# Attention followed by a two-layer Mish network: the first layer of the last two token groups as seven products in place of eight

## The chip, the core and the metric

The kernel runs on one core of one Trainium2 chip. TensorE (PE) multiplies matrices and writes its results to PSUM, which has eight banks; VectorE (DVE), ScalarE (ACT) and GpSimd (POOL) work on tiles; SyncE (SP) issues DMA transfers. Every engine runs its own instructions in order and waits on semaphores for the others. The metric is the device time of one execution in microseconds. All times below are microseconds unless another unit stands beside them.

## What is computed

Linear attention with a decay per head, in blocks of 64 positions, on 4 batches, 8 heads, 768 positions and 64 channels; its output, rearranged to 3072 tokens of 512 channels, goes through a network 512 to 2048 to 512 with the Mish function between the layers:

```python
for b in range(nb):                                  # blocks of 64 positions
    intra = np.einsum('bhic,bhjc->bhij', qb, kb) * Dmask[None]
    intra = np.einsum('bhij,bhjd->bhid', intra, vb)
    inter = np.einsum('bhid,bhde->bhie', qb * lam_pow[None], kv_state)
    out[:, :, sl] = intra + inter
    kv_state = lam_block[None, :, None, None] * kv_state + np.einsum('bhsd,bhse->bhde', kb_dec, vb)
...
x = np.ascontiguousarray(attn_out.transpose(0, 2, 1, 3)).reshape(B * S, H * D)
h = x @ w_in                                         # (3072, 512) @ (512, 2048)
sp = np.where(h > 20.0, h, np.log1p(np.exp(np.minimum(h, 20.0))))
g = h * np.tanh(sp)
return (g @ w_out).astype(np.float32)                # (3072, 2048) @ (2048, 512)
```

## The kernel before

The positions are cut into six groups of 128 (n = 0 to 5); a group has 512 tokens, 128 of each batch. Three things are done for a group, each in a later stage than the one before: attention, the first layer with Mish, and the second layer. The order of all instructions is written out by hand, and each engine and each DMA queue takes its own in that order.

**Attention of a group** goes by batch b. `scores` (L246) multiplies the transposed keys and queries kT and qT into the banks be and bo, and DVE multiplies them by the decay mask into two tiles sb (L255). `outputs` (L267) multiplies the queries by the running state and the masked scores by the values into bank bz; DVE scales that into xn (L279), and SP transposes xn by DMA into xt (L282), the input of the first layer, with tokens along its free side. `state` (L294) renews the running state: PE into bank be, DVE adds (raw, L305), POOL multiplies (L307). `turn_dma` (L235) makes kT and qT of two batches by DMA transposes; the tiles rotate over three buffers each. `load_pair` (L84) loads k, q, v, issued by POOL.

**First layer.** A `unit` (L332) makes 128 of the 2048 hidden features of a group: four matmuls over the 512 inputs, weights of win as the stationary side, 512 tokens moving (L324), into one of the banks bA, bB, bC in turn; ACT applies Mish from there into hsg (L330). A group has 16 units. The weights lie in four tiles win[0] to win[3], each with 512 of the features. For group 1, `two_units` (L343) does the same with 256 tokens at a time.

**Second layer.** For groups 1 to 5 it is done with seven products in place of eight: tokens, hidden features and output features are cut in halves, and sums of quarters (`token_sum`, L379, on the activations; `weight_sum`, L366, on the weights wout) are multiplied instead of the quarters. `dense2` (L437) does the products in the order 1, 2, 6, 5, 7, 3, 4, each as two half products of eight matmuls with 256 columns (L431), in the banks bG and bH: the value after product 1 is copied by ACT from bG to bH and grows on in both, and ACT and DVE make the four output quarters from them. `dense2_alone` (L489) does it for the last group, with more banks and nothing beside it.

**The loop** (L715, n = 1 to 4) interleaves, on PE, the attention of group n+2 (`s_` for the scores, `o_` for outputs and state), the 16 units of group n+1 (`u`) and the half products of group n (`h`). In turn n = 3 the last attention, of group 5, is done, without a new state; turn n = 4 has no attention. The last two half products that a turn calls already belong to the group after. The tail after the loop is `dense2_alone` for group 5.

## Time and profile before

| | |
|---|---|
| median of 3 runs | 210.7 us (210.14 to 212.43) |
| profiled execution | 210.12 us, its span 208.4 us |
| instructions in the span | 4263 |
| mean granted TensorE clock | 0.994 |

The span reaches from the first to the last instruction that the profile shows; the rest of the time lies around it. In rows of groups the numbers are the busy time, the mean duration in ns of one instruction, and the idle time of the engine just before them with what ended it. In rows of the timeline they are start, duration, engine, line and operation; the idle time before stands in brackets. In rows of stretches they are the length, then busy time and instruction count of each engine, the granted TensorE clock, the share of the DMA engines, and GB/s. Consecutive matmuls overlap: in the timeline a run of them is shown longer than the distance to the next one's start; the chain of waits shows that distance.

### The profile page before, as it was taken

What the parts mean: (1) busy time and instruction counts of PE and PEld (TensorE: products, weight loads), DVE (VectorE), ACT (ScalarE), POOL (GpSimd) and SP (SyncE); (2) the same over time, 40 slices, a digit from 0 to 9 for tenths busy, and PEclk for the clock granted to TensorE, in tenths of its full rate; (3) what the DMA queues carried; (4) which work ended last, traced back from release to release, by engine and by line L of the source; (5) the groups of instructions that cost most, each with busy time, mean ns of one, the idle gap of its engine ahead of it and who ended that gap; (6) DMA issues with size and microseconds to landing.
All of it is one profiled execution on the core that took longest, in us unless ns stands there. A gap on an engine that the chain in (4) does not pass through costs nothing.

```text
span 208.4 us, 4263 instructions
## 1 busy us (share of the span) xinstructions
PE 196.9 (94%) x1783; PEld 134.1 (64%) x1783; DVE 124.9 (60%) x201; ACT 89.4 (43%) x154; POOL 70.8 (34%) x68
## 2 busy tenths in 40 slices
PE   7568998999999999999999999999999999999991
PEld 3455555788855566667766657766667666666891
DVE  6656758785957957657965657951638340153341
ACT  4674586648421124442254342344352354525300
POOL 7997553531292540763411665400000000000020
PEclk9999999999999999999999999999999999999997
DMA  9999999999989999999991999992022401012033
GB/s 131 136 170 205 162 179 157 182 206 179 160 95 173 203 150 170 140 146 98 194 265 56 73 116 176 159 234 78 3 25 76 129 0 50 0 53 101 0 104 101
DMA packets 109301, 26.23 MB, mean 126 GB/s; under 512 B 99426, under 2 KB 108770, under 8 KB 109282
## 3 DMA queue, kind: packets, MB, share of 16 engines
q0 software_dynamic: 77536, 13.37, 83.3%
q1 hardware_dynamic: 30704, 12.33, 29.7%
q10 hardware_dynamic: 1042, 0.26, 0.6%
q8 instruction: 14, 0.23, 0.4%
q14 instruction: 5, 0.04, 0.1%
HBM read 27.26 MB, written 6.29 MB: 161 GB/s over the span
## 4 chain that ended last, share of the span: by engine, by line
PE 88%; DMA 4%; POOL 2%; ACT 2%; DVE 1%; issue 1%; POOLq 0%; DVEq 0%
PE bG L431 15%; PE bH L431 13%; PE bA L324 11%; PE bB L324 11%; PE bC L324 11%; DMA qn<-in_q_dram 3%; PE be L251 3%; PE bB L350 3%; PE bz L271 2%; PE bz L276 2%; PE bA L350 2%; PE bC L350 2%; PE bA L482 2%; PE bG L482 2%; PE bC L482 2%; PE bB L482 2%
## 5 line engine op out<-in xcount | busy, mean ns | idle before, releaser
L324 PEld LDWEIGHTS <-win 128*128 128x128 f16 x328 | 30.5, 98 | 24.0 <-issue 1.0
L307 POOL TENSOR_TENSOR w<-raw,lbm 128x512 f16<-128x512 f32 x14 | 20.4, 1458 | 53.7 <-DVE raw L305 53.7
L431 PEld LDWEIGHTS <-gsum 128*128 128x128 f16 x336 | 30.9, 98 | 7.3
L431 PEld LDWEIGHTS <-hsg 128*128 128x128 f16 x240 | 23.4, 98 | 7.8
L324 PE MATMUL bA<-xt,win 128*128 128x512 f16 (+2 forms) x112 | 27.9, 371 | 0.6 <-ACT xt L265 0.6
L324 PE MATMUL bC<-xt,win 128*128 128x512 f16 x108 | 27.7, 379 | 0.0
L255 DVE TENSOR_TENSOR sb<-be,dm 128x512 f16<-128x512 f32 x23 | 15.8, 688 | 18.8 <-PE bo L251 18.8
L324 PE MATMUL bB<-xt,win 128*128 128x512 f16 (+2 forms) x108 | 26.9, 371 | 0.0
L330 ACT ACTIVATE hsg<-bA 128x512 f16<-128x512 f32 x27 | 16.1, 597 | 24.4 <-PE bA L324 24.4
L330 ACT ACTIVATE hsg<-bB 128x512 f16<-128x512 f32 x26 | 15.5, 598 | 23.6 <-PE bB L324 23.6
L279 DVE TENSOR_TENSOR xn<-bz,lq 128x512 f16<-128x512 f32 x20 | 13.8, 692 | 18.9 <-PE bz L276 18.9
L330 ACT ACTIVATE hsg<-bC 128x512 f16<-128x512 f32 x27 | 16.2, 598 | 20.3 <-PE bC L324 20.2
L513 POOL TENSOR_TENSOR u<-u,u 128x512 f32<-128x512 f32 x1 | 1.3, 1274 | 64.2 <-DVE u L512 64.2
L431 PE MATMUL bH<-tsum,gsum 128*128 128x256 f16 x160 | 20.4, 273 | 0.0
L431 PE MATMUL bG<-wout,hsg 128*128 128x256 f16 x160 | 20.2, 272 | 0.0
L394 DVE TENSOR_TENSOR gsum<-hsg 128x1024 f16<-128x1024 f16 x20 | 15.1, 753 | 6.4 <-ACT hsg L330 6.4
L255 DVE TENSOR_TENSOR sb<-bo,dm 128x512 f16<-128x512 f32 x23 | 15.7, 681 | 0.0
L244 DVE TENSOR_TENSOR kd<-kn,lk 128x512 f16<-128x512 f16 x20 | 14.7, 741 | 0.0
L350 PEld LDWEIGHTS <-win 128*128 128x128 f16 x128 | 12.1, 98 | 1.8
L459 DVE TENSOR_TENSOR u<-bH,r 128x512 f32<-128x512 f32 x4 | 2.8, 692 | 17.3 <-ACT r L457 17.3
L87 POOL DMA_DIRECT2D kn<-in_k_dram x10 | 11.8, 1183 | 2.9 <-DVE kd L244 1.5
L87 POOL DMA_DIRECT2D vn<-in_v_dram x10 | 11.6, 1161 | 2.3 <-DMA win<-in_moe_w_in_dram 1.4
(123 smaller groups left out, 294.3 us busy)
## 6 DMA issues: line engine op xcount, KB each, us to landing
out_dram<-osum SPq DMA_DIRECT2D x23, 256.0 KB, 2.3
kn<-in_k_dram POOLq DMA_DIRECT2D x11, 256.0 KB, 9.1
qn<-in_q_dram POOLq DMA_DIRECT2D x11, 256.0 KB, 6.8
vn<-in_v_dram POOLq DMA_DIRECT2D x10, 256.0 KB, 8.4
wout<-in_moe_w_out_dram POOLq DMA_DIRECT2D x4, 512.0 KB, 15.4
win<-in_moe_w_in_dram POOLq DMA_DIRECT2D x3, 512.0 KB, 11.1
vz<-in_v_dram POOLq DMA_DIRECT2D x2, 256.0 KB, 6.6
k<-in_k_dram SPq DMA_DIRECT2D x1, 256.0 KB, 3.3
```

The lines of the kernel that those rows point to most:

```text
L87: nc.gpsimd.dma_start(out=tile_, in_=rows(src, n, 2 * bp, 2))
L244: eng.tensor_tensor(out=kd[n, b], in0=kn[n, b], in1=bc(lk, 2, D), op=ALU.mult)
L251: nc.tensor.matmul(p_[t][:, j, :], kT[n, b][rs, j, :], qT[n, b][rs, j, :], start=True, stop=True)
L255: nc.vector.tensor_tensor(out=sb[n, b, t], in0=p_[t], in1=dm[:, t], op=ALU.mult)
L279: nc.vector.tensor_tensor(out=xn, in0=po, in1=bc(lq, 2, D), op=ALU.mult)
L307: decay = lambda: eng.tensor_tensor(out=w_new, in0=raw, in1=lbm, op=ALU.mult)
L324: nc.tensor.matmul(open_[n, ni][:, lo:hi], win[ni // 4][:, kc, (ni % 4) * 128 : (ni % 4) * 128 + 128], xt[n][:, kc, lo:hi], start=(opens a ...
L330: nc.scalar.activation(h_tile(n)[:, ni, :], open_.pop((n, ni)), AF.Mish)
L350: nc.tensor.matmul(t[:, u, :], win[ni // 4][:, kc, m : m + 128], xt[n][:, kc, cs], start=(u == 0 and kc == 0), stop=(kc == NKC - 1), skip_ ...
L394: nc.vector.tensor_tensor(out=gsum[n, i][:, ks, :], in0=a, in1=b, op=op)
L431: nc.tensor.matmul(t, lhs(kk, blk), rhs(kk)[:, lo:hi], start=(fresh and kk == 0), stop=(kk == HK - 1), skip_group_check=True)
L482: nc.tensor.matmul(po, hsg[n][:, ki, b * C : (b + 1) * C], wout[part][:, kk, :], start=(ki == 0), stop=(ki == NKI - 1))
```

## The change

Groups 4 and 5, that is turns n = 3 and n = 4 of the loop, get their first layer by seven products instead of eight. What belongs to one win tile (512 features) of a group is one set. Its 2 x 2 quarters are: the two halves of the features, and the two halves of the tokens; the 512 inputs are cut in halves too. Each product is four matmuls with 256 columns, and three banks are used:

- Product 1 goes into the first bank (a); ACT copies it into the second (b, step "seed"). Product 2 is added onto a, from which ACT makes the first quarter's Mish.
- Product 5 goes into the third bank (c); ACT copies it to SBUF (p5).
- Product 6 is added onto b; DVE writes b + p5 into c.
- Product 7 is added onto b; DVE writes b + p5 to SBUF (c22), from which ACT makes another quarter's Mish.
- Product 3 is added onto c and product 4 onto b; ACT makes the last two quarters' Mish from there.

The products need sums of weight quarters (`wsum`, four for each win tile) and of input quarters (`xsum`, four for each group). DVE makes the sixteen weight sums in turns 1 and 2, the input sums at the start of turns 3 and 4. Turns 1 and 2 keep their units.

In turn 3 the sets run one after another in the banks A, B, C, with B and C exchanged in every second set; product 4 of a set is left over until the next set has begun, and one half product of the second layer (in two sets with the outputs of a batch) stands between products 6 and 7. In turn 4, two sets run in step, one in A, B, C and one in the attention's banks e, z, o.

The tiles kT and qT get two buffers instead of three, `turn_dma` for the group after stands ahead of a unit and a score block instead of behind them, and two temporaries of `dense2_alone` take the names (and so the space) of p5 and c22.

```diff
-                turned[name, n] = work.tile([128, 2 * JP, C], F16, name=name, tag=name, bufs=3)
+                turned[name, n] = work.tile([128, 2 * JP, C], F16, name=name, tag=name, bufs=2)
...
-            tile_ = work.tile([128, 2 * JP, C], F16, name=f"{t}T", tag=f"{t}T", bufs=3)
+            tile_ = work.tile([128, 2 * JP, C], F16, name=f"{t}T", tag=f"{t}T", bufs=2)
...
+    wsum = [const.tile([128, 4, 2, HC], F16, name=f"wsum{s}") for s in range(WS)]
+
+    def w_sum(s, i, eng):
+        w, t = win[s], wsum[s]
+        a, b_, op = (
+            (w[:, 0:2, HC:], w[:, 2:4, HC:], ALU.add),
+            (t[:, 0], w[:, 0:2, 0:HC], ALU.subtract),
+            (w[:, 0:2, 0:HC], w[:, 0:2, HC:], ALU.subtract),
+            (w[:, 2:4, 0:HC], t[:, 1], ALU.subtract),
+        )[i]
+        eng.tensor_tensor(out=t[:, i], in0=a, in1=b_, op=op)
...
+    def x_sums(n, *which):
+        x = xt[n]
+        t = xsum.setdefault(n, {})
+        for i in which:
+            t[i] = work.tile([128, 2, HC], F16, name=f"xsum{i}", tag=f"xsum{i}", bufs=1)
+            a, b_ = (
+                lambda: (x[:, 0:2, HC:], x[:, 0:2, 0:HC]),
+                lambda: (x[:, 2:4, HC:], t[0]),
+                lambda: (x[:, 2:4, HC:], x[:, 0:2, HC:]),
+                lambda: (x[:, 2:4, 0:HC], t[1]),
+            )[i]()
+            nc.vector.tensor_tensor(out=t[i], in0=a, in1=b_, op=ALU.subtract)
+
+    def set_of(n, s, banks):
+        o = Set()
+        o.n, o.s, o.banks = n, s, banks
+        o.home = ("raw", "raw", 2) if banks[0] == "e" else ("p5", "c22", 1)
+        return o
+
+    def seven(o, i, t, fresh):
+        w, x, ws, xs = win[o.s], xt[o.n], wsum[o.s], xsum.get(o.n)
+        for u in range(2):
+            for kk in range(2):
+                us = slice(u * 128, u * 128 + 128)
+                lhs, rhs = (
+                    lambda: (w[:, kk, us], x[:, kk, 0:HC]),
+                    lambda: (w[:, 2 + kk, us], x[:, 2 + kk, 0:HC]),
+                    lambda: (ws[:, 3, kk, us], x[:, 2 + kk, HC:]),
+                    lambda: (w[:, 2 + kk, HC + u * 128 : HC + u * 128 + 128], xs[3][:, kk, :]),
+                    lambda: (ws[:, 0, kk, us], xs[0][:, kk, :]),
+                    lambda: (ws[:, 1, kk, us], xs[1][:, kk, :]),
+                    lambda: (ws[:, 2, kk, us], xs[2][:, kk, :]),
+                )[i - 1]()
+                nc.tensor.matmul(t[:, u, :], lhs, rhs, start=(fresh and u == 0 and kk == 0),
+                                 stop=(kk == 1), skip_group_check=True)
+
+    def mish(o, r, t, src):
+        nc.scalar.activation(
+            h_tile(o.n)[:, 4 * o.s + 2 * r : 4 * o.s + 2 * r + 2, t * HC : t * HC + HC], src, AF.Mish)
+
+    def set_step(o, step):
+        if step == "m1":
+            o.a = bank(o.banks[0], [2, HC])
+            seven(o, 1, o.a, True)
+        elif step == "seed":
+            o.b = bank(o.banks[1], [2, HC])
+            nc.scalar.activation(o.b, o.a, AF.Copy)
+        elif step == "m2":
+            seven(o, 2, o.a, False)
+            mish(o, 0, 0, o.a)
+        elif step == "m5":
+            o.c = bank(o.banks[2], [2, HC])
+            seven(o, 5, o.c, True)
+            o.p5 = work.tile([128, 2, HC], F32, name="p5", tag=o.home[0], bufs=o.home[2])
+            nc.scalar.activation(o.p5, o.c, AF.Copy)
+        elif step == "m6":
+            seven(o, 6, o.b, False)
+            nc.vector.tensor_tensor(out=o.c, in0=o.b, in1=o.p5, op=ALU.add)
+        elif step == "m7":
+            seven(o, 7, o.b, False)
+            o.c22 = work.tile([128, 2, HC], F32, name="c22", tag=o.home[1], bufs=o.home[2])
+            nc.vector.tensor_tensor(out=o.c22, in0=o.b, in1=o.p5, op=ALU.add)
+        elif step == "m3":
+            seven(o, 3, o.c, False)
+            mish(o, 0, 1, o.c)
+        elif step == "m4":
+            mish(o, 1, 1, o.c22)
+            seven(o, 4, o.b, False)
+            mish(o, 1, 0, o.b)
...
-        u3, u2 = keep("u3"), keep("u2")
+        u3, u2 = keep("p5"), keep("c22")
...
+    KINDS = {1: "pppp", 2: "pppp", 3: "ssss", 4: "ssss"}
+    WSUMS = {(1, 0): (0,), (1, 1): (2,), (2, 0): (1,), (2, 1): (3,)}
```

The loop's body for turn 3 ("s") and turn 4 (`m >= NG`), with the branches of turns 1 and 2 left out; there the order is the one of before, with `ws(n, 0)` behind `sums(n, 1, 2, 3)`, `ws(n, 1)` behind `u(5)` and `turn_dma(m + 1, 0)` ahead of `u(4)`:

```python
        for i, x in enumerate((0, 2, 1, 3)):
            spare = ("e", "z", "o") if m >= NG else ("A", "C", "B")
            alone = (("A", "B", "C"), spare)
            turn = i % 2 if kinds[i - 1] == "s" else 0
            sets.append(set_of(n + 1, x, alone[turn]) if kinds[i] == "s" else None)
        def settle():
            while owed:
                mm(owed.pop(), "m4")
        def opening(i):
            if kinds[i] == "s":
                mm(i, "m1")
                s_(i)
                mm(i, "seed")
                if i != 1:
                    settle()
...
        def closing(i):
            mm(i, "m7", "m3")
            owed.append(i)
        if m >= NG:                       # turn 4; both(i, ...) calls a step for sets i and i + 1
            x_sums(n + 1, 0, 1, 2, 3); sums(n, 1, 0, 1)
            both(0, "m1", "seed"); h(1)
            both(0, "m2", "m5"); h(1)
            both(0, "m6"); h(1)
            both(0, "m7"); sums(n, 1, 2, 3); both(0, "m3"); h(1)
            both(0, "m4"); h(2)
            both(2, "m1", "seed", "m5", "m2"); h(1)
            both(2, "m6"); sums(n + 1, 0, 0, 1); h(1)
            both(2, "m7"); h(1); sums(n + 1, 0, 2)
            both(2, "m3"); h(1); sums(n + 1, 0, 3)
            both(2, "m4"); h(2)
            continue
        x_sums(n + 1, 0, 1, 2, 3)         # turn 3
        opening(0); turn_dma(m, 1); h(1)
        mm(0, "m2", "m5", "m6"); sums(n, 1, 0, 1); h(1); o_(0); closing(0)
        opening(1); h(1); settle(); mm(1, "m2"); h(1)
        mm(1, "m5", "m6"); sums(n, 1, 2); h(1); o_(1); closing(1)
        opening(2); sums(n, 1, 3); h(1)
        mm(2, "m2", "m5", "m6"); o_(2); h(1); closing(2); h(1)
        sums(n + 1, 0, 0, 1); h(1)
        opening(3); h(1); mm(3, "m2", "m5"); h(1); mm(3, "m6"); o_(3); h(1)
        mm(3, "m7", "m3"); owed.append(3); sums(n + 1, 0, 2, 3)
        halves = dense2(n + 1); h(1); h(1); settle()
```

More of the change, by code (lines that the diff above doesn't have):

```diff
@@ L741 @@
+        if "s" in kinds:
+            x_sums(n + 1, 0, 1, 2, 3)
+        opening(0)
         if m < NG:
             turn_dma(m, 1)
[L743 to L763 removed]
@@ L764 @@
-        h(1)
-        u(11)
-        h(1)
-        u(4)
-        s_(2)
+        if kinds[0] == "s":
+            h(1)
+            mm(0, "m2", "m5", "m6")
+            sums(n, 1, 0, 1)
+            h(1)
+            o_(0)
+            fetch(("k", 0), ("q", 0))
+            closing(0)
+        else:
+            u(0)
+            sums(n, 1, 0, 1)
+            if n == 1:
+                weight_sum(3, 0)
+                weight_sum(3, 1)
+            h(1)
+            u(1)
+            h(1)
+            u(2)
+            o_(0)
+            fetch(("k", 0), ("q", 0))
+            u(3)
@@ new lines @@
+        opening(1)
+        h(1)
+        if kinds[1] == "s":
+            settle()
+            mm(1, "m2")
+            h(1)
+            mm(1, "m5", "m6")
+            sums(n, 1, 2)
+            h(1)
+            o_(1)
+            fetch(("v", 0), ("k", 1))
+            closing(1)
+        else:
+            u(8)
+            settle()
+            s_(1)
+            sums(n, 1, 2, 3)
+            ws(n, 0)
+            h(1)
+            u(9, 10)
+            o_(1)
+            fetch(("v", 0), ("k", 1))
+            h(1)
+            u(11)
@@ new lines @@
+        opening(3)
+        if kinds[3] == "s":
+            h(1)
+            mm(3, "m2", "m5")
+            h(1)
+            mm(3, "m6")
+            o_(3)
+            h(1)
+            mm(3, "m7", "m3")
+            owed.append(3)
+            sums(n + 1, 0, 2, 3)
+        else:
+            s_(3)
+            h(1)
+            u(12)
+            settle()
+            h(1)
+            o_(3)
+            u(13)
+            sums(n + 1, 0, 2, 3)
+            h(1)
+            u(14)
+        more = n + 1 < NG - 1
```

120 lines of the change are left out of this document (79 added, 41 removed).

## The prediction

> **What bounds the kernel now.** I read the page first, then the busy time in each turn of the late loop, then the chain that ended last. The page says that TensorE is busy almost throughout, and that it carries the chain.
>
> ```profile
> span 208.4 us, 4263 instructions
> ...
> PE 196.9 (94%) x1783; PEld 134.1 (64%) x1783; DVE 124.9 (60%) x201; ACT 89.4 (43%) x154; POOL 70.8 (34%) x68
> ...
> PE 88%; DMA 4%; POOL 2%; ACT 2%; DVE 1%; issue 1%; POOLq 0%; DVEq 0%
> ```
>
> Below are the loop's turns n = 1 (with the two half products ahead of it), 2, 3, 4 and the tail, cut about where the first matmul of each starts.
>
> ```profile
> core 0: us, PE busy (x) PEld busy (x) DVE busy (x) ACT busy (x) POOL busy (x), PEclk, DMA share, GB/s
> 75.04:106.70 31.66, 31.66 (x285) 21.54 (x284) 22.39 (x33) 12.04 (x21) 12.75 (x11) 1.00 1.70 157
> 106.70:137.72 31.02, 31.02 (x278) 20.80 (x275) 20.59 (x30) 12.28 (x21) 12.74 (x10) 1.00 1.36 147
> 137.72:167.25 29.53, 29.53 (x258) 19.72 (x258) 14.84 (x24) 11.93 (x20) 0.00 (x0) 1.00 0.30 71
> 167.25:191.56 24.31, 24.31 (x162) 15.64 (x160) 7.71 (x12) 11.33 (x19) 0.00 (x0) 1.00 0.10 33
> 191.56:208.40 16.84, 12.44 (x129) 11.17 (x127) 5.38 (x11) 2.39 (x4) 1.27 (x1) 0.93 0.23 79
> ```
>
> In turns 3 and 4 PE never idles, at full clock, so a removed matmul is worth its whole length unless a new wait takes its place. The chain inside turn 4 gives the lengths, and the earlier `two_units` show the shape that the new products have:
>
> ```profile
> 39.44 0.87 PE bB L350 x8
> ...
> 170.91 0.86 PE bB L324 x4
> 171.77 0.86 PE bC L324 x4
> 172.63 0.87 PE bH L431 x8
> ```
>
> A unit (4 matmuls of 512 columns) costs 0.86; 8 matmuls of 256 columns cost 0.87, with win as weights (L350) as with the second layer's operands (L431). So a new product (2 x 2 matmuls of 256) costs 0.435, and a half product of the second layer, called a half below, 0.87.
>
> **What is removed.** In each of turns 3 and 4, 16 units go (16 x 0.86 = 13.76) and 4 sets x 7 products x 4 = 112 matmuls of 256 columns come (14 x 0.87 = 12.18). That is 1.58 a turn, 3.16 in all: turn 3 from 29.53 to 27.95, turn 4 from 24.31 to 22.73 if nothing waits. That is the best case. The 14 and 12 halves stay, and turn 3's attention of group 5 too (29.53 - 13.76 - 12.18 = 3.59, about 0.42 for a score block and 0.48 for an output block).
>
> **What is added on ACT and DVE.** A unit had one Mish; a set has four, plus two copies (seed, p5) on ACT and two adds (after products 6 and 7) on DVE. The nearest rows:
>
> ```profile
> L330 ACT ACTIVATE hsg<-bC 128x512 f16<-128x512 f32 x27 | 16.2, 598 | 20.3 <-PE bC L324 20.2
> ...
> L459 DVE TENSOR_TENSOR u<-bH,r 128x512 f32<-128x512 f32 x4 | 2.8, 692 | 17.3 <-ACT r L457 17.3
> ...
> L457 ACT ACTIVATE r<-bG 128x512 f32<-128x512 f32 x4 | 2.4, 597 | 1.1 <-PE bG L431 1.1
> ...
> L450 ACT ACTIVATE bH<-bG 128x512 f32<-128x512 f32 x4 | 2.3, 582 | 2.3 <-PE bG L431 2.3
> ...
> L233 DVE COPY qT<-bz 128x512 f16<-128x512 f16 x2 | 0.8, 420 | 1.4 <-PE bz L225 1.4
> ```
>
> ACT gains 8 x 0.6 = 4.8 a turn: 16.7 of 27.95 and 16.1 of 22.73. DVE gains 8 adds of 0.69 and four input sums (at 0.42, priced below), 7.2 a turn: 22.0 of 27.95 and 14.9 of 22.73. Neither becomes the bound by amount; what matters is latency, because PE needs the seed before product 2, the first add before products 7 and 3, the second before product 4. The add after product 6 writes PSUM, which no DVE row does. ACT's rows put PSUM output at 582 against 597 for SBUF, so I take 0.69, the row with the same operation and size; the ends are 0.42, the copy's, and 1.38, twice the row.
>
> The Trainium skill, "ScalarE: Activation LUTs", section "Step-by-step: what each stage is for", speaks against the change here: ACT lies nearer to PSUM, VectorE nearer to SBUF. The ACT rows agree, by 15 ns; mirrored to DVE (my estimate) that is 8 x 0.015 = 0.12 us in all, and the gain summed below would be 2.54 instead of 2.66.
>
> **The hand-offs.** In the order of time: ACT's pitch, ACT to PE, PE to ACT:
>
> ```profile
> 19.68 0.60 ACT L330 ACTIVATE hsg<-bA 128x512 f16<-128x512 f32 x1 [0.47 <-PE bA L324]
> 20.18 0.59 ACT L330 ACTIVATE hsg<-bB 128x512 f16<-128x512 f32 x1
> ...
> 35.30 0.62 ACT L231 ACTIVATE qT<-bz 128x512 f16<-128x512 f16 x1
> ...
> 35.97 0.38 PE L271 MATMUL bz<-w,qT 128*128 128x128 f16 x4 [0.62 <-ACT qT L231]
> ...
> 169.01 1.03 PE L324 MATMUL bA<-xt,win 128*128 128x512 f16 x4
> ...
> 170.07 0.60 ACT L330 ACTIVATE hsg<-bA 128x512 f16<-128x512 f32 x1 [1.17 <-PE bA L324]
> ```
>
> A unit issued from 169.01 to 169.87 is read from 170.07: 0.20. ACT starts every 0.50 when work waits. PE goes on 0.05 after ACT's end.
>
> Set 0 of turn 3, from its start, with a score block at 0.42 and an output block at 0.46 (0.02 less than above, which is the harder case for the waits): product 1 to 0.44, scores to 0.86, half to 1.73. The seed runs behind the second layer's own copy, 0.67 to 1.25, so product 2 (1.73) is free. Mish 2.37 to 2.97, p5 2.87 to 3.47, first add 3.50 to 4.18. PE meanwhile does products 2, 5, 6, the half that was put between 6 and 7, and the output block, to 4.37; product 7 needs 4.23: 0.14 to spare. The second add stands behind two token sums and xn on DVE, 6.02 to 6.70; product 4 comes at 6.98: 0.23 to spare. In the same way product 7 of the other sets has 0.21, 0.08 and over 0.4 to spare, product 4 0.13 or more, product 5 (which waits for the bank of the set before) 0.2 or more. So turn 3 is free by these rows, with little to spare. The cover is the half and the output block: without them product 7 would stand 1.2. At 1.38 for the first add (0.69 more) product 7 stands 0.55, 0.48, 0.61 and 0.29 in turn 3 and about 0.3 twice in turn 4, 2.5 in all.
>
> Turn 4 has no attention, and two sets in step cover each other: 0.4 or more to spare at every product 7, save at its opening. There ACT still has the second layer's copy and two Mish of the last set in its queue (ends 0.4, 0.9 and 1.4 after the turn's start), then the seeds (1.9 and 2.4). PE is at product 2 after two products and a half, 1.75: it waits 0.14 and 0.05, about 0.2 in all. The half between reads the last Mish with its seventh matmul, 0.1 after it ended; were its first matmul held, 0.5 more. The input sums need xt; first the time of its transpose to landing, then DVE's last work before turn 3:
>
> ```profile
> xt<-xn SPq DMA_TRANSPOSE x16, 2.8
> ```
>
> ```profile
> 134.20 1.76 DVE L394 TENSOR_TENSOR gsum<-hsg,gsum 128x1024 f16<-128x1024 f16 x1
> ```
>
> In turn 4 the last xn ends 2.9 before the turn; with 2.8 for the transpose the input sums start at its start and product 5 comes 2.8 later. In turn 3 they fill DVE's idle time from 135.96.
>
> **Sixteen weight sums**, four behind the scores of block 1 and four behind those of block 2, in turns 1 and 2. The tight place, in turn 2:
>
> ```profile
> 124.14 0.68 DVE L255 TENSOR_TENSOR sb<-bo,dm 128x512 f16<-128x512 f32 x1
> 126.06 0.69 DVE L279 TENSOR_TENSOR xn<-bz,lq 128x512 f16<-128x512 f32 x1 [1.24 <-PE bz L276]
> 126.67 0.68 DVE L305 TENSOR_TENSOR raw<-be,w 128x512 f32<-128x512 f32 x1
> ...
> 127.87 1.39 DVE L394 TENSOR_TENSOR gsum<-hsg 128x1024 f16<-128x1024 f16 x1
> 129.29 0.69 DVE L394 TENSOR_TENSOR gsum<-gsum,hsg 128x1024 f16<-128x1024 f16 x1
> ...
> 131.10 0.68 DVE L255 TENSOR_TENSOR sb<-bo,dm 128x512 f16<-128x512 f32 x1
> ...
> 131.97 0.40 PE L276 MATMUL bz<-vn,sb 128*128 128x64 f16 x8
> ```
>
> Free operations start 0.61 apart (126.06, 126.67), 0.08 before the last one ends; a dependent one 0.03 after the end (129.26, 129.29). A sum of 512 fp16 pairs lies between 0.34, half of what one of 1024 takes (129.29), and 0.69, the whole; I take the 0.42 of the 512 fp16 copy, the nearest in size and type. Four then start 0.34 apart, one of them 0.45 (the second waits for the first), 1.47 where 1.33 are free (124.73 to 126.06), and push xn by 0.14. DVE has no gap from there to the sb that ends at 131.78, and PE reads that at 131.97: 0.19 less a hand-off of 0.05 just covers it, so I cost them at nothing. At 0.69 each (4 x 0.61 + 0.1) they push 1.2 and PE would stand 1.05, in each of the two turns. The first four of a turn have PE waits behind them that are microseconds away. POOL's multiply and loads behind raw slip as much and are used a turn later.
>
> **Two buffers for kT and qT instead of three.** A turn's transpose now waits for the output block two tiles back. That is over before the transpose starts, so it costs nothing:
>
> ```profile
> 87.71 0.39 PE L271 MATMUL bz<-w,qT 128*128 128x128 f16 x4
> ...
> 90.38 1.25 SPq L238 DMA_TRANSPOSE kT<-kn  x1
> ```
>
> It is moved ahead of a unit and a score block; SP's own order (half's store, then kT and qT) stays.
>
> **The sum.** 3.16 - 0.2 (opening of turn 4) - 0.3 (a dozen hand-offs with 0.08 to 0.25 to spare, whose latencies I know to about 0.1) = 2.66. The profiled run took 210.12 (span 208.4 and 1.7 around it); 210.12 - 2.66 = 207.46, so **207.5**. The median of the runs shown, 210.7, lies 0.6 higher; the same difference would make 208.1.
>
> **Rivals.** (a) Hand-offs are longer than the rows say, the add that writes PSUM above all: at its upper end 2.5 more, 210.0; at half of that 1.25 more, 208.7, which I take. For it: product 7 has 0.08 to 0.21 to spare in three sets of turn 3. Against: PE idles nowhere in turns 1 to 3, with the same kind of chain in the second layer. (b) The weight sums cost 0.68: 2.1 more, 209.6. Against: the copy's 0.42. (c) Slower: in turn 3 the first add comes behind two more DVE operations (1.2) in each set, because DVE, 79% full, has run late; product 7 stands 1.05, four times, 4.2 in all: 211.7. It decides from 0.66 a set. If product 4 waits too, 8.4, 215.9. Against: the adds lie ahead of token sums in DVE's order. (d) Freed time is not kept, the tail waiting for the last Mish: about 210.1. Against: the last Mish ends before the tail starts. (e) The clock falls because PE pauses between groups:
>
> ```profile
> 202.30:208.40 6.10, 1.70 (x24) 1.45 (x21) 1.57 (x4) 0.00 (x0) 0.00 (x0) 0.80 0.30 98
> ```
>
> That stretch, with PE busy 1.70 of 6.10, was granted 0.80; 50.7 us of the two turns at 0.80 would be 12.7 longer, 220. Turns with PE busy all the time have 1.00, and the pauses that I expect are 0.2. The Trainium skill, "TensorE: Matmul & The Clock Gate", section "A second HAM failure mode: psum-queue depth-cycling", says that short idles between groups that cycle through PSUM banks can throttle the clock; the four turns above, which cycle through banks, do not show it.
>
> **How the numbers follow.** Forecast (206.9 to 208.0) 0.58; (a) 0.24; (b) 0.06; (c) 0.07, of which 0.04 beyond 1%; (d) 0.03; (e) 0.02. A measurement of this kernel tells about 1%, 2.1 us, from no change: faster is the forecast's 0.58; same is (a), (b), (d) and 0.03 of (c), 0.36; slower 0.06. The range goes from 206.9 (nothing waits) to 209.7 (most of (a), all of (b)) and leaves out 0.12 above.
>
> **What would show it.** Turn 3 near 28.0 to 28.3 and turn 4 near 22.9 to 23.2, PE idle under 0.5 in both; a wait for ACT's seed at the opening of turn 4; xn of turn 2's block 2 about 0.1 later, and no wait at L276 of block 3. Wrong it would be by PE waits for the DVE adds (product 7) or by ACT falling behind in turn 3.

## The result and the profile after

| | before | after |
|---|---|---|
| median (lowest to highest), 6 runs each, same chip | 210.5 (210.02 to 212.43) | 207.88 (207.24 to 210.78) |
| ratio, 95% interval | | 0.986 [0.9816, 0.9905] |
| profiled execution | 210.12 | 207.71 |
| its span | 208.4 | 205.8 |

By the ratio of the means the kernel became faster by 1.4%, with an interval from 0.95% to 1.8%; by the medians it is 1.2%. The ratio leaves out the slow execution of 210.78 after (granted clock 0.98), and keeps the 212.43 of before. The same kernel measured once more gave 208.21 against 210.18, 0.9907 [0.9877, 0.9937]. Both intervals lie below 1, and the size of the gain lies near 1%.

The head of the page of the changed kernel; instructions and busy time of each engine:

```profile
span 205.8 us, 4537 instructions
...
PE 195.8 (95%) x1879; PEld 145.1 (70%) x1879; DVE 142.5 (69%) x241; ACT 95.9 (47%) x170; POOL 70.7 (34%) x68
```

DVE took on 17.6 (124.9 to 142.5) and ACT 6.5. PE lost only 1.1 of busy time over the whole span: 2.9 in turns 3 and 4, while the stretch before turn 1 shows 1.6 more in this execution. The stretches below are cut, and their columns are, as those of before: turn 1 with the two half products ahead of it, turns 2, 3, 4 and the tail.

```profile
75.10:106.70 31.60, 31.60 (x284) 21.43 (x282) 24.95 (x41) 11.93 (x20) 12.99 (x11) 1.00 1.64 155
106.70:137.98 31.28, 31.28 (x282) 21.17 (x279) 23.55 (x39) 12.52 (x21) 12.72 (x10) 1.00 1.31 151
137.98:166.02 28.04, 28.04 (x306) 24.33 (x304) 20.98 (x36) 14.63 (x27) 0.00 (x0) 1.00 0.27 68
166.02:188.99 22.97, 22.91 (x211) 20.30 (x209) 14.11 (x25) 15.02 (x29) 0.00 (x0) 1.00 0.11 38
188.99:205.80 16.81, 12.43 (x130) 11.16 (x127) 4.94 (x11) 2.39 (x4) 1.27 (x1) 0.94 0.24 81
```

Turn 3 went from 29.53 to 28.04 and turn 4 from 24.31 to 22.97: 1.49 and 1.34 less, together 2.83. The tail gained 0.03, and turn 3 starts 0.26 later in this execution, which leaves 2.60, the difference of the spans. That 0.26 is there before the loop begins. The next two fences, before and then after, show the stretch from the first score block of turn 1 to the start of turn 3:

```profile
76.72:137.72 61.00, 61.00 (x545) 41.02 (x544) 42.97 (x63) 23.86 (x40) 25.46 (x20) 1.00 1.51 152
```

```profile
77.03:137.98 60.95, 60.95 (x546) 41.13 (x545) 48.50 (x80) 23.86 (x40) 25.43 (x20) 1.00 1.45 153
```

It starts 0.31 later and takes 0.05 less. DVE carries the sixteen weight sums in it, 5.5 more, and PE is busy all the time. The changed kernel and its variants below with the same work up to that point begin turn 1 anywhere from 76.36 to 77.54, the kernel before at 76.72, so such an offset belongs to an execution and not to the change. The loop alone, turns 1 to 4, went from 114.84 (76.72 to 191.56) to 111.96 (77.03 to 188.99): 2.88 less.

Turn 3's 28.04 is 0.09 above its floor of 27.95, but that is the cut. The rows around the turn's start, before and then after:

```profile
137.41 0.38 PE L431 MATMUL bG<-wout,hsg 128*128 128x256 f16 x2
137.73 0.23 PE L251 MATMUL be<-qT,kT 64*128 64x128 f16 x1
```

```profile
137.98 0.60 PE L407 MATMUL bA<-xt,win 128*128 128x256 f16 x4
138.51 0.23 PE L251 MATMUL be<-qT,kT 64*128 64x128 f16 x1
```

Two matmuls take 0.22 and four 0.44, so each score block starts 0.10 later than the matmuls ahead of it explain. Before, the turn began with a score block and this step lay ahead of the cut; now product 1 begins the turn and the step lies inside. Nothing in turn 3 waits.

Three places were named beforehand. The first is the gap ahead of product 7 (timeline; the first add writes the bank, product 7 comes after it). Set 0 of turn 3:

```profile
141.50 0.70 DVE L432 TENSOR_TENSOR bC<-bB,p 128x512 f32<-128x512 f32 x1 [1.17 <-ACT p L429]
...
142.15 0.40 PE L276 MATMUL bz<-vn,sb 128*128 128x64 f16 x8
142.38 0.60 PE L407 MATMUL bB<-xsum,wsum 128*128 128x256 f16 x4
```

The add ends at 142.20, 0.18 ahead of product 7, which has no wait in brackets; in set 2 the two are 0.13 apart (154.52 and 154.65). Take 0.05 off for the hand-off, and 0.13 and 0.08 were to spare.

The second is the opening of turn 4:

```profile
166.86 0.59 ACT L411 ACTIVATE hsg<-bC 128x512 f16<-128x512 f32 x1
166.89 1.04 PE L518 MATMUL bG<-wout,hsg 128*128 128x256 f16 x8
...
167.34 0.60 ACT L421 ACTIVATE bB<-bA 128x512 f32<-128x512 f32 x1
...
167.85 0.56 ACT L421 ACTIVATE bz<-be 128x512 f32<-128x512 f32 x1
...
167.99 0.60 PE L407 MATMUL bA<-xt,win 128*128 128x256 f16 x4
...
168.47 0.60 PE L407 MATMUL be<-xt,win 128*128 128x256 f16 x4
```

The half product ends at 166.89 + 0.87 = 167.76. Product 2 of the two sets starts at 167.99 and, instead of 0.44 later, 0.48 later: waits of 0.23 and 0.04. Each starts 0.05 or 0.06 after its seed (L421) ends, and the seeds stand behind two Mish (L411) of the last set in ACT's queue, the second of which is shown.

The third is block 2 and 3 of turn 2, with the first of four weight sums (L370):

```profile
125.09 0.41 DVE L370 TENSOR_TENSOR wsum<-win 128x512 f16<-128x512 f16 x1
...
126.55 0.68 DVE L279 TENSOR_TENSOR xn<-bz,lq 128x512 f16<-128x512 f32 x1
...
131.57 0.68 DVE L255 TENSOR_TENSOR sb<-bo,dm 128x512 f16<-128x512 f32 x1
...
132.31 0.40 PE L276 MATMUL bz<-vn,sb 128*128 128x64 f16 x8
```

The four take 1.46 (125.09 to 126.55). xn comes 0.49 later than before, 0.35 of which the whole block does (sb, 124.14 and 124.49); that leaves a push of 0.14. The last sb ends at 132.25, and L276 reads it at 132.31 without a wait.

### The profile page after: what moved, and what is told of

It reads as the page before. It is cut to its first block, busy times and chain, and to the rows that moved or that the text cites. A ratio compares the mean times of both kernels' runs of the same rounds, so it can differ in the third digit from the quotient of the medians.

```text
span 205.8 us, 4537 instructions
## 1 busy us (share of the span) xinstructions
PE 195.8 (95%) x1879; PEld 145.1 (70%) x1879; DVE 142.5 (69%) x241; ACT 95.9 (47%) x170; POOL 70.7 (34%) x68
## 4 chain that ended last, share of the span: by engine, by line
PE 78%; DMA 9%; POOL 8%; DVE 1%; ACT 1%; issue 1%; POOLq 0%; DVEq 0%; ACTq 0%
PE bG L518 15%; PE bH L518 13%; DMA qn<-in_q_dram 8%; PE bA L324 5%; PE bC L324 5%; PE bB L324 4%; PE bB L407 3%; PE bC L407 3%; PE be L251 3%; PE bB L350 3%; PE bA L407 2%; PE bA L350 2%; PE bC L350 2%; POOL win L96 2%; PE bz L276 2%; PE bz L271 2%
## 5 line engine op out<-in xcount | busy, mean ns | idle before, releaser
L324 PEld LDWEIGHTS <-win 128*128 128x128 f16 x200 | 18.3, 98 | 14.6 <-issue 1.0
L600 POOL TENSOR_TENSOR c<-p,u 128x512 f32<-128x512 f32 x1 | 1.3, 1275 | 61.2 <-DVE p L599 61.2
L324 PE MATMUL bA<-xt,win 128*128 128x512 f16 (+2 forms) x72 | 17.6, 367 | 0.6 <-ACT xt L265 0.6
L330 ACT ACTIVATE hsg<-bA 128x512 f16<-128x512 f32 x17 | 10.2, 597 | 13.9 <-PE bA L324 13.9
L324 PE MATMUL bC<-xt,win 128*128 128x512 f16 x64 | 16.4, 379 | 0.0
L330 ACT ACTIVATE hsg<-bB 128x512 f16<-128x512 f32 x15 | 9.0, 598 | 14.6 <-PE bB L324 14.6
L324 PE MATMUL bB<-xt,win 128*128 128x512 f16 (+2 forms) x64 | 15.6, 366 | 0.0
L330 ACT ACTIVATE hsg<-bC 128x512 f16<-128x512 f32 x16 | 9.6, 597 | 11.4 <-PE bC L324 11.3
L350 PEld LDWEIGHTS <-win 128*128 128x128 f16 x128 | 12.1, 98 | 1.8
L407 PEld LDWEIGHTS <-wsum 128*128 128x128 f16 x128 | 12.4, 98 | 1.4
```

The lines of the kernel that those rows point to most:

```text
L324: nc.tensor.matmul(open_[n, ni][:, lo:hi], win[ni // 4][:, kc, (ni % 4) * 128 : (ni % 4) * 128 + 128], xt[n][:, kc, lo:hi], start=(opens a ...
L330: nc.scalar.activation(h_tile(n)[:, ni, :], open_.pop((n, ni)), AF.Mish)
L350: nc.tensor.matmul(t[:, u, :], win[ni // 4][:, kc, m : m + 128], xt[n][:, kc, cs], start=(u == 0 and kc == 0), stop=(kc == NKC - 1), skip_ ...
L407: nc.tensor.matmul(t[:, u, :], lhs, rhs, start=(fresh and u == 0 and kk == 0), stop=(kk == 1), skip_group_check=True)
```

## The experiments

My theory: in turns 3 and 4 PE is the only limit, so what goes is the length of the removed columns, 1.58 a turn; what was put between products 6 and 7 covers the chain over ACT and DVE; the weight sums fit into DVE's gaps, just. The rivals: the gain comes from elsewhere (other names, two buffers, the moved transposes), the cover is not needed, or the sums are paid for.

**Turn 4 alone, and turn 3 alone.** The new first layer in one of the two turns only; weight sums, buffers and the moved steps stay.

```diff
-    KINDS = {1: "pppp", 2: "pppp", 3: "ssss", 4: "ssss"}
+    KINDS = {1: "pppp", 2: "pppp", 3: "pppp", 4: "ssss"}
```

> Turn 3 goes back to 16 units, turn 4 keeps the sets in step. Theory (a removed column is worth its length on PE, the sets' hand-offs are covered): turn 3 back at 29.5, turn 4 about 23.0 without the wait at its opening, or a little less; the whole 1.3 to 1.6 faster than before, 1.3 to 1.5 slower than the changed kernel. Rival (the gain comes from the two turns together, or from one of them alone): turn 4 at 24.3, or all of the 2.6 here.

```diff
-    KINDS = {1: "pppp", 2: "pppp", 3: "ssss", 4: "ssss"}
+    KINDS = {1: "pppp", 2: "pppp", 3: "ssss", 4: "pppp"}
...
-        if m >= NG:
+        if m >= NG and kinds[0] == "s":
```

> Turn 3 keeps its four sets one after another, turn 4 goes back to 16 units. Theory: turn 3 at 28.0, turn 4 at 24.3; the whole 1.3 to 1.6 faster than before. With the kernel that has turn 4 alone the two gains add up to that of the change. Rival: turn 3 as long as before (29.5), its sets paying for their hand-offs.

Measured: 208.92 against 210.46 (0.9934 [0.9897, 0.997]), and 209.35 (0.9951 [0.9919, 0.9983]). Turns 3 and 4, first with turn 4 alone changed, then with turn 3 alone:

```profile
138.50:168.01 29.51, 29.51 (x257) 19.70 (x257) 16.34 (x28) 11.93 (x20) 0.00 (x0) 1.00 0.34 67
168.01:190.74 22.73, 22.73 (x211) 20.34 (x209) 12.94 (x21) 14.18 (x27) 0.00 (x0) 1.00 0.10 33
```

```profile
137.60:165.64 28.04, 28.04 (x307) 24.33 (x305) 21.10 (x35) 14.65 (x27) 0.00 (x0) 1.00 0.28 73
165.64:189.93 24.29, 24.29 (x163) 15.61 (x161) 7.76 (x12) 12.04 (x21) 0.00 (x0) 1.00 0.11 38
```

Each turn gains by itself: turn 4 comes to 22.73, the removed columns to the hundredth (24.31 - 1.58), and turn 3 to 28.04. The turn that kept its units stays within 0.02 of its old length, so the names, buffers and moved transposes do nothing there. With turn 3 on units, turn 4 has no wait at its opening: ACT has a single Mish there, begun at 167.34 and over before the turn starts. The medians say the same more coarsely: 1.54 and 1.11 less than before, the second below the 1.3 to 1.6 that was expected.

**The cover taken away.** In all four sets of turn 3 the half product that stands between products 6 and 7 goes behind product 3. The work is the same.

```diff
             mm(0, "m2", "m5", "m6")
             sums(n, 1, 0, 1)
-            h(1)
             o_(0)
             fetch(("k", 0), ("q", 0))
             closing(0)
+            h(1)
```

> In the four sets of turn 3 the half product that stood between products 6 and 7 stands behind product 3; nothing is added or taken away. Theory (this half and the output block cover p5 on ACT and the first add on DVE): product 7 stands 0.73, 0.66, 0.79 and 0.47 in the four sets, turn 3 goes from 28.0 to about 30.7, which takes the whole gain of the change: about the time of before. Rival (the output block alone covers them, or PE has work that fills the gap): turn 3 under 28.5.

Measured: 210.36 against 210.46, 0.9993 [0.9964, 1.0022]. Turn 3, the waits of PE in it, and the first product 7 from the timeline:

```profile
138.00:168.82 30.82, 28.68 (x307) 24.58 (x304) 21.56 (x37) 14.49 (x27) 0.00 (x0) 1.00 0.25 62
```

```profile
PE bB L407 <- DVE bC L432: 1.2, 2, 0.6
PE bC L407 <- DVE bB L432: 0.9, 2, 0.5
```

```profile
142.27 0.60 PE L407 MATMUL bB<-xsum,wsum 128*128 128x256 f16 x4 [0.58 <-DVE bC L432]
```

Turn 3 takes 2.78 more, as much as the whole change gains, so the same half product is worth 0.7 a set where it stands. The waits view names the first add alone. Its 2.1 are less than 2.78 because idle time is counted from the modelled end of the matmuls ahead. By the starts, L276 began at 141.30 here and takes 0.23 to the next start (142.15 to 142.38 in the changed kernel); product 7 could have started at 141.53 and started at 142.27, 0.74 later, where the bracket has 0.58. Four times the 0.16 between them is 0.64, the growth of PE's busy time from 28.04 to 28.68.

**The last product 4 a half product earlier.** At the end of turn 3, so that ACT is done with the last Mish sooner.

```diff
+            settle()
             if more:
                 h(1)
-            settle()
```

> At the end of turn 3 product 4 of the last set goes ahead of the second half product of group 4, so that its two Mish stand ahead of the second layer's copy in ACT's queue and the seeds of turn 4 come earlier. Theory (the 0.3 that PE waits at the opening of turn 4 comes from ACT's queue): product 2 waits for no seed any more, turn 4 goes from 22.97 to about 22.7, the whole 0.3 faster than the changed kernel. Rival (the seeds are late because their products 1 are): the wait stays at 0.3.

Measured: 207.45 (207.14 to 209.03), 0.9862 [0.9821, 0.9903]. The opening of turn 4:

```profile
166.62 1.03 PE L518 MATMUL bG<-wout,hsg 128*128 128x256 f16 x8
166.96 0.59 ACT L421 ACTIVATE bz<-be 128x512 f32<-128x512 f32 x1
167.49 0.60 PE L407 MATMUL bA<-xt,win 128*128 128x256 f16 x4
```

Product 2 follows the half product without a wait, and turn 4 (165.73 to 188.46) takes 22.73. So the 0.24 above 22.73 in the changed kernel is ACT's queue at the opening and nothing else. In the medians 0.2 cannot be told from the change itself.

**Turn 4 with one set after another**, by the path of turn 3 (which then finds no attention to place).

```diff
-        if m >= NG:
+        if False:
```

> Turn 4 does its sets one after another in the order of turn 3 (banks A, B, C and e, z, o by turns), without the output and score blocks that stand there in turn 3. Theory (two sets in step cover each other's way through ACT and DVE; one set alone has only one half product, 0.87, and product 6, 0.44, against 1.6 from the end of product 5 to the end of the first add): product 7 stands about 0.3 in each of the four sets, product 2 about 0.6 at the opening, turn 4 at 24.2 to 24.6 instead of 22.97, so that the gain of turn 4 is gone; the whole 1.2 to 1.6 slower than the changed kernel. Rival (the halves cover a set alone as well): turn 4 under 23.2.

Measured: 209.91 against 210.34, 1.0 [0.997, 1.0029]. Turn 4:

```profile
167.61:192.89 25.28, 24.09 (x210) 20.21 (x208) 13.00 (x22) 15.09 (x29) 0.00 (x0) 1.00 0.12 40
```

2.31 more than in step, and more than the 24.31 of the units. All six banks are still in use here, by sets in turn; what is gone is the second set beside the first, and without it seven products lose to eight in this turn. I had the direction right and the size too small. Counted by starts, as above, PE is held at nine places by 0.11 to 0.51, 2.58 in all, against the 2.55 by which the turn exceeds 22.73: 0.64 at the opening, for the last Mish and the seed, 0.93 at the four product 7s for the first add, 0.37 for the second layer's add, 0.64 at two product 4s for the second add. The last one:

```profile
192.46 0.60 PE L407 MATMUL bz<-xsum,win 128*128 128x256 f16 x4 [0.34 <-DVE c L436]
```

By the starts it is 0.51: product 3 ahead of it began at 191.51 and takes 0.44. The gain of turn 4 thus rests on the two sets in step as much as on the seven products.

**The weight sums doubled.** In each of turns 1 and 2 the four sums of the second place are made twice.

```diff
-            for x in WSUMS.get((n, i), ()):
+            for x in WSUMS.get((n, i), ()) * (1 + i):
```

> The second four weight sums of turns 1 and 2 are made twice (eight in place of four behind the scores of block 2); the output is the same. Theory (they are free only because DVE's gap of 1.3 holds four of them; the sb of block 3 is then ready just as PE comes to it): four more push DVE's chain by 1.47, and PE stands 1.4 at the output block of batch 3 in each of the two turns, 2.8 in all: about 210.6. Rival (DVE has more slack behind them): under 0.5 in all.

Measured: 210.79 against 210.34, 1.001 [0.9975, 1.0045]. Turns 1 and 2 together, then the first of the waits:

```profile
77.54:141.36 63.82, 61.74 (x545) 41.43 (x545) 51.34 (x88) 23.85 (x40) 25.47 (x20) 1.00 1.45 146
```

```profile
103.02 0.68 DVE L255 TENSOR_TENSOR sb<-bo,dm 128x512 f16<-128x512 f32 x1
103.16 0.10 PEld L276 LDWEIGHTS <-sb 128*128 128x128 f16 x1 [0.67 <-DVE sb L255]
```

63.82 against 60.95: four more sums of 0.42 in each turn cost 1.4 a turn, at L276 of block 3. So four sums fit at that place, and what comes on top is paid for in full: the sums are free because DVE's gap there is as long as they are.

**More of the same: turn 2 as well.** Five kernels carry the sets into turn 2. The first does sets 2 and 3 by products; the weight sums must then be made earlier, eight of them in one place.

```diff
-    KINDS = {1: "pppp", 2: "pppp", 3: "ssss", 4: "ssss"}
-    WSUMS = {(1, 0): (0,), (1, 1): (2,), (2, 0): (1,), (2, 1): (3,)}
+    KINDS = {1: "pppp", 2: "ppss", 3: "ssss", 4: "ssss"}
+    WSUMS = {(1, 0): (0, 1), (1, 1): (2,), (2, 0): (3,)}
```

> The last two sets of turn 2 (group 3) by seven products as well, the weight sums for them made one place earlier. Theory (PE bound): turn 2 loses 0.8 of its 31.2, less what DVE makes late: DVE has 23.6 there now and gets 1.7 of input sums and 2.8 of adds, 28.0 of 30.5, and POOL's multiplies hold it up besides; turn 2 between 30.4 and 31.2. Rival (DVE becomes the bound of that turn): turn 2 above 31.3, the whole not faster than the changed kernel.

The second does set 3 alone and leaves the weight sums where they were.

```diff
-    KINDS = {1: "pppp", 2: "pppp", 3: "ssss", 4: "ssss"}
+    KINDS = {1: "pppp", 2: "ppps", 3: "ssss", 4: "ssss"}
```

> Only the last set of turn 2 by seven products as well. Theory: turn 2 loses 0.4 of its 31.2 (four units of 0.86 for 28 matmuls of 256 columns, 3.05), DVE at 26.6 of 30.8 still keeps up: 30.8 to 31.0. Rival: DVE's input sums at the start of the turn and the adds at its end make PE wait 0.5 or more: turn 2 at 31.3 or above.

Measured: 207.98 (0.9887 [0.9858, 0.9917]) and 208.46 (0.9914 [0.9886, 0.9942]): no gain on the change. With two sets turn 2 lost its 0.84, as it should, but turn 1 got 0.6 longer (PE waits for sb behind the eight sums) and turn 3 went from 28.04 to 28.87. DVE at the start of turn 3 in that kernel, and in the changed kernel:

```profile
139.15 0.42 DVE L385 TENSOR_TENSOR xsum<-xt 128x512 f16<-128x512 f16 x1 [1.76 <-DMA xt<-xn]
...
141.82 0.69 DVE L432 TENSOR_TENSOR bC<-bB,p 128x512 f32<-128x512 f32 x1
```

```profile
137.58 0.43 DVE L385 TENSOR_TENSOR xsum<-xt 128x512 f16<-128x512 f16 x1 [1.26 <-DMA xt<-xn]
...
141.50 0.70 DVE L432 TENSOR_TENSOR bC<-bB,p 128x512 f32<-128x512 f32 x1 [1.17 <-ACT p L429]
```

In the changed kernel DVE is free for 1.17 before the first add. With two sets in turn 2, PE begins turn 3 at 137.33, 0.65 earlier, yet xt lands 1.57 later; the four input sums, both sb and the first add then follow without a gap, and product 7 of set 0 comes at 142.56, 5.23 after the start of the turn instead of 4.40. That is the 0.83. With one set, turn 2 from its first score block takes 30.42 (107.05 to 137.47) against the changed kernel's 30.45, but 0.34 of it is a wait of PE for xt at its start; without that it lost the forecast 0.4. Turn 3 takes 28.91 there, for the same reason as with two sets: the sums start at 139.33, 1.86 after the turn's start.

The third spreads the weight sums (eight of them ahead of the loop), puts the last output block of a turn earlier, so that the last xn is made earlier, and takes the earlier product 4 from above.

```diff
+    for t in range(4):
+        w_sum(0, t, nc.vector)
...
+    for t in range(4):
+        w_sum(2, t, nc.vector)
...
-    KINDS = {1: "pppp", 2: "pppp", 3: "ssss", 4: "ssss"}
-    WSUMS = {(1, 0): (0,), (1, 1): (2,), (2, 0): (1,), (2, 1): (3,)}
+    KINDS = {1: "pppp", 2: "ppss", 3: "ssss", 4: "ssss"}
+    WSUMS = {(1, 0): (1,), (2, 0): (3,)}
...
             mm(3, "m2", "m5")
+            o_(3)
             h(1)
             mm(3, "m6")
-            o_(3)
```

> From the kernel with product 4 moved ahead at the end of a turn: the last two sets of turn 2 by seven products too; the weight sums of win tiles 0 and 2 stand ahead of turn 1, where DVE idles 2.2 and 2.6, those of tile 1 and 3 behind the scores of block 1 of turns 1 and 2, none behind block 2; in the last set of a turn the outputs of batch 3 come ahead of the half before product 6, 1.3 earlier. Theory (with two sets more in turn 2, turn 3 lost 0.8 because its input sums waited for the last transpose of xt, and turn 1 lost 0.6 to eight weight sums in one place): turn 1 at 30.5, turn 2 at 29.6, turn 3 at 28.0 to 28.3, turn 4 at 22.7; the whole about 1.0 faster than the changed kernel, 206.8. Rival (DVE's amount of work in turn 2 is what makes turn 3 start late): turn 3 stays at 28.7 or above, the whole within 0.3 of the changed kernel.

Measured: 208.0, 0.9883 [0.9857, 0.991]. Turns 2 and 3, and a piece of the chain from 130 to 141 (start, length, what):

```profile
107.53:137.30 29.77, 29.77 (x298) 22.95 (x298) 24.67 (x43) 13.71 (x24) 12.76 (x10) 1.00 1.36 126
137.30:167.21 29.91, 28.70 (x306) 24.32 (x304) 21.60 (x37) 15.68 (x28) 0.00 (x0) 1.00 0.40 86
```

```profile
132.61 7.32 DMA xt<-xn
```

Turn 2 is as wanted, so are turns 1 and 4 (30.50 and 22.72), and turn 3 is 1.9 too long; PE waits 0.8 for the first input sum in it. My theory, that xn is made too late, fell: the transpose was issued at 132.61, 1.7 earlier than with two sets and unspread sums (134.31), and landed at 139.93, later.

Two more start from the third. The fourth does all of turn 2 by products, the fifth issues the last loads of q and v a block earlier, in case these loads hold the transpose up.

```diff
-    KINDS = {1: "pppp", 2: "ppss", 3: "ssss", 4: "ssss"}
-    WSUMS = {(1, 0): (1,), (2, 0): (3,)}
+    KINDS = {1: "pppp", 2: "ssss", 3: "ssss", 4: "ssss"}
+    WSUMS = {(1, 0): (1,), (1, 1): (3,)}
```

> As the one before, with all four sets of turn 2 by seven products (weight sums of tile 3 behind block 2 of turn 1). Theory (DVE bound: 20.6 in that turn before, 7.2 more is 27.8 of 28.9, with POOL's multiplies in its way and the input sums of group 3 at its start behind a transpose that lands about when the turn begins): PE waits for DVE in turn 2, which stands between 29.2 and 30.2, and the whole is no faster than with two sets. Rival (PE bound still): turn 2 at 28.9 to 29.1, the whole 0.6 faster than with two sets.

```diff
-            fetch(("v", 0), ("k", 1))
+            fetch(("v", 0), ("k", 1), ("q", 1), ("v", 1))
...
-            fetch(("q", 1), ("v", 1))
```

> The kernel with two sets in turn 2 and spread weight sums, with the last two loads of a turn (q and v of batches 2 and 3 of the group after next) issued one block earlier, behind block 1 instead of block 2, about 5 earlier. Theory (the last transpose of xt, issued at 132.6, landed only at 139.9 because the DMA engines were full of those loads; the input sums of turn 3 wait for it): it lands by 137, turn 3 goes from 29.9 to 28.0 to 28.4, turn 2 stays at 29.6 to 29.8, the whole at 206.5 to 207.0, 1.0 faster than the change. Rival (the transpose is slow for another cause, its place in the SP queue or its own packets): it lands at 139 or later, turn 3 above 29, the whole within 0.3 of the change.

Measured: 207.72 (0.9883 [0.9856, 0.9909]) and 208.21 (206.77 to 211.05; 0.9895 [0.9851, 0.9939]). With four sets turn 2 takes 30.64, longer than with two and than the 29.2 to 30.2 expected, and in it PE waits 0.9 for the add of the new state; xt lands at 138.6. With the loads earlier the transpose is issued at 135.35 and the first input sum starts at 142.44, in an execution that is 1.9 late before turn 1 and 2.2 late from turn 2 on: 7.1, as long as with the loads at their old place. But the edit did less than it was meant to. POOL issues the two loads at 127.43 and 128.56, against 127.68 and 128.88 in the kernel it starts from; less the 2.2 that is 2.5 earlier and not 5, and the packets of the loads run on until 139.3. So this run does not clear the loads; the last section comes back to them.

**The change once more.** The unaltered changed kernel, with another profile.

> The changed kernel itself once more, for comparison on the same chip: 207.9, 0.986 to 0.989 of the kernel before; turn 3 at 28.0, turn 4 at 23.0; the input sums of turn 3 start within 1.0 of the first matmul of that turn.

Measured: 208.21 (207.52 to 209.5), 0.9907 [0.9877, 0.9937], a little less gain than expected. Its profiled execution is the longest of its runs, 209.5, and shows why. Turns 2 and 3, then the start of turn 2:

```profile
107.31:139.53 32.22, 30.47 (x273) 20.63 (x273) 23.80 (x40) 11.93 (x20) 12.76 (x10) 1.00 1.31 155
139.53:167.58 28.05, 28.05 (x307) 24.32 (x305) 20.85 (x35) 14.63 (x27) 0.00 (x0) 1.00 0.26 67
```

```profile
102.72 1.22 SPq L282 DMA_TRANSPOSE xt<-xn  x1
...
109.45 1.04 PE L324 MATMUL bA<-xt,win 128*128 128x512 f16 x4 [1.75 <-DMA xt<-xn]
```

Turns 3 and 4 repeat within 0.01 (turn 4 takes 22.96). The whole excess is one wait of 1.75 in turn 2, whose units the change leaves as they were, for a transpose of xt that took 6.7 from issue to use.

This wait is no single case. Of the seven profiles of kernels with the changed turns 1 and 2, four have it, with 0.56 (turn 4 alone), 0.65 (the half product moved), 1.57 (one set after another) and 1.75 (here); in the other three it is 0.2 at most by the starts. The one profile of before has none, though its transpose is issued just as late, 25.89 after the first score block of turn 1 against 25.91. The times point the same way: of 51 executions of these kernels at a granted clock of 0.99 or more, 7 lie 1.6 to 2.5 above the fastest of their kernel; of 67 of the kernel before, none lies more than 1.35 above the fastest on its chip. So the changed kernel seems to meet this wait more often and to lose part of its gain to it. What brings it about (weight sums, two buffers, moved transposes) was not tried one by one.

No version beat the change by more than its measurement can tell. The nearest is the one with the earlier product 4, whose turns 3 and 4 take 28.03 and 22.73, their floors.

## Why the prediction was right

The time came out at 207.88 where 207.5 was forecast, inside the likeliest case's own range. The sum of 2.66 is to be held against the span's 2.60 and the medians' 2.62, and the loop by itself gained 2.88. That the total fits better than its parts is in part luck, as the points below show, and in the second measurement, whose profile shows a wait in turn 2 that the prediction did not have, the medians differ by 1.97 only. The 0.4 between forecast and median is the difference, named beforehand, between the profiled execution (210.12) and the median of before (210.5).

- *The removed columns, 3.16.* Right to the hundredth in turn 4: 22.73 was the floor, and 22.73 stands there in the two kernels without the opening's wait. Turn 3's floor of 27.95 came out at 28.04, by 0.09 that only moved over the cut. The loop's 2.88 is, within 0.01, 3.16 less the opening's 0.27.
- *The opening of turn 4, 0.2.* 0.27 by the starts, 0.24 by the turn's length, for the cause given: the seeds behind two Mish in ACT's queue. Moving product 4 removed it.
- *What ACT and DVE take on, 4.8 and 7.2 a turn.* Oversized: ACT's busy time rose by 2.7 and 3.7 in turns 3 and 4, DVE's by 6.1 and 6.4. The sum took every operation at its full length, but operations that follow at once overlap (ACT's two seeds start 0.51 apart, and the first takes 0.60). Nothing in the time hung on it.
- *Hand-offs, 0.3.* Oversized: they cost nothing. What took the place of this 0.3 in the span's difference is the 0.31 by which this execution was late before the loop, which the prediction did not have and which is chance. The gaps ahead of product 7, forecast at 0.14 and 0.08 for sets 0 and 2, measured 0.13 and 0.08.
- *The add that writes PSUM, 0.69 between 0.42 and 1.38.* 0.70. The by-form groups of the changed kernel, the add into PSUM, the add into SBUF, and the weight sum:

```profile
L370 DVE TENSOR_TENSOR wsum<-win 128x512 f16<-128x512 f16 x8 | 3.3, 416 | 0.0
...
L432 DVE TENSOR_TENSOR bC<-bB,p 128x512 f32<-128x512 f32 x4 | 2.8, 699 | 6.9 <-PE bB L407 5.4 <-ACT p L429 1.5
L436 DVE TENSOR_TENSOR c<-bB,p 128x512 f32<-128x512 f32 x4 | 2.7, 686 | 0.6 <-PE bB L407 0.6
```

  The forms differ by 13 ns. The Trainium skill, "ScalarE: Activation LUTs", section "Step-by-step: what each stage is for", has VectorE nearer to SBUF than to PSUM; the 699 against 686 ns agree in sign, and no wait in turns 3 and 4 hangs on them.
- *The cover.* The prediction called the half product and the output block the cover and priced its loss at about 1.2 a set without both. Moving the half product alone cost 0.7 a set, the whole gain.
- *Sixteen weight sums at nothing.* 0.42 each, a push of 0.14, and no wait at L276, all three as forecast. Doubling them shows that the gap is just that long: four more cost 1.4 a turn.
- *Input sums.* Here a step was mis-sized. I gave the transpose of xt 2.8 from issue to landing, the page's median, and let the sums fill DVE's idle time from 135.96. In turn 3 they started at 137.58, 4.1 after the issue at 133.47. It cost nothing, because 1.17 of DVE's time was still free ahead of the first add; from about 1.3 later on (with the 0.13 at product 7) it would have, as two sets in turn 2 show: there the sums come 2.2 later against the turn's start, and 0.83 is lost. For turn 4 the 2.5 measured (163.22 to 165.72) fits.
- *The rivals.* (a) and (b) fall with 0.70 and 0.42. (c), adds that come late on DVE in turn 3, did not happen here, but with late input sums it is what turn 2 by products ran into. (d) falls: the tail takes 16.81 against 16.84. (e) falls: the clock is 1.00 in turns 3 and 4. The two buffers for kT and qT and the moved transposes show no wait of their own, but neither was tried by itself, and whether the wait for xt in turn 2 hangs on them is open.

The chance of 0.58 for more than 1% was near the edge: 1.4% in one measurement, 0.9% in the other.

## What to carry to other kernels

On an engine that never idles, a removed instruction is worth its length, and its chain of helpers costs nothing only if work that is needed anyway is put into each gap: count the cover of each step as carefully as the gain, since one half product in the wrong place of each set took all of it back. A step that is free now is free by a stated slack (0.08 at a product 7 and 0.01 at L276 once the hand-off is taken off, 1.17 ahead of the first add); write these numbers down, because the next change of the same kind meets them first. For a DMA in a stage whose DMA engines are full, take the spread of its landings and not the median.

## What was not expected of the hardware

The transposes of xt had no fixed time to landing. From issue to the first use that waited for it, the last one of group 4, in turn 2, took 4.1 and 3.8 in the two profiles of the changed kernel, 4.8 with two sets in turn 2, 6.0 with four, 7.4 and 7.1 in the two spread variants with two sets, while the one of group 5, in turn 3, took 2.5. Issued anywhere from 132.6 to 135.1, the one of group 4 was used no earlier than 137.4. The busy tenths of the DMA engines, in 40 slices of the span, for the changed kernel and then for the one with spread sums:

```profile
DMA  9999999999969999799994399992212221003123
```

```profile
DMA  9999999999989999799996299992212121003123
```

The 9s end with slice 27 of 40, at about 139, in both; behind them the row stands at 0 to 3, and the transpose of 2.5 lies there. But the transpose of the changed kernel is used at 137.58, while the engines are still full. The split by queues says more. From 133 to 135, with the transpose issued at 133.47, one queue has all the packets (packets, MB, share of 16 engines, above 100% because packets in flight together are added up):

```profile
q0 software_dynamic: 2387, 0.30, 237.6%
```

I take q0 for the loads that POOL issues: in this trace it has no packet from 136 to the end, and POOL's last load is issued at 130.33. The other large queue, q1, starts again at 135.0, q0 ends at 135.9, and the transpose is used 1.7 later. In the second profile q0 has nearly all the packets from 135 to 137 and ends at 137.2, and the use is 1.7 later too, at 138.86. My reading is that the transpose runs only when the packets of the loads have run out, so shortening turn 2 only makes PE meet it earlier. It is not the whole: with sets in turn 2 the use comes 2.7 to 3.2 after nearly all of q0's packets, and the further 1.0 to 1.5 has no cause shown. No run here removed the loads from this stretch.
